# Six matmuls on a zero tile, in three places of the opening of a fused SSM-convolution and SwiGLU kernel

## The chip, the cores and the metric

The kernel runs on one core of a Trainium2 chip. A core has a matmul engine (PE), a vector engine (DVE), an activation engine (ACT), a general one (POOL), a queue engine for DMAs (SP), an on-chip memory of 128 partitions, and a small accumulator memory (PSUM) that PE writes and DVE and ACT read. The metric is the device time of one execution in microseconds. It was measured in four runs: median 284.02 us, from 283.33 to 284.58.

## The reference

Inputs are bfloat16; the sequence has 2048 rows of 640 channels. Cut to what matters:

```python
x = A_q
q = layernorm(x)
k_shift = sum over t in 0..3 of k[row - t] * shift_k[:, t]      # a causal filter with four taps
kv = k_shift * v
y = irfft(rfft(kv, 4096) * rfft(ssm_k, 4096))[:2048]           # a causal convolution along the rows
h = x + q * (y + kv * ssm_D)
n = layernorm(h)
out = h + (silu(n @ w_gate) * (n @ w_up)) @ w_down              # inner width 1728
```

## The kernel before, in words

The 2048 rows are worked on as four blocks of 512 (NB, MB), the 640 channels as the free dimension. The long convolution is done block by block with trigonometric transforms written as matmuls: the filter blocks are transformed by WG (g_transform), the products kv by WX (x_transform), pairs of transformed blocks are multiplied on DVE (pair), and WI goes back (inverse). Each block then goes through layernorm and the feed-forward part (ffn).

The kernel builds a list of operations, each with an engine, what it reads and writes, and a function that issues its instructions (Plan.add). Operations are numbered in the order in which the code adds them. The list SEQUENCE, written out in full, gives the order in which they are issued. Each engine works through its own operations in that order; between engines, an instruction waits for those it depends on. PSUM is split into two pools, A and F, of two buffers each (psA, psF), each of two banks; an operation with acq takes the buffer that was released longest ago, and one with rel gives it back.

What happens in the opening, with its lines:

- Line 278 clears the tile junk (the same memory as hl[0]) on DVE, and warm (lines 282 to 290) issues five matmuls 128x512 on it, then one DVE copy of a single element that reads the result.
- wcast (lines 321 to 329), four times: two matmuls each spread one row of the four-tap filter over all partitions, into pool A, and ACT copies the result to w4.
- gload(0) (line 302 on): the first filter block is loaded, and transposed by PE as matmuls against an identity (line 314), five to a group, four groups, in pool F; ACT copies each group out (line 316).
- front_first (line 379 on), for each tile of 128 rows of the first block: DVE multiplies k by the four filter rows (line 383), PE adds up the shifted rows with band matrices, the taps (line 393), into pool A, and for the first two tiles turns v around (line 401). DVE multiplies both (lines 404, 406). SP's loads of the next block's k come into tiles that the taps read, and so wait for them.
- g_transform(0) (line 344) and x_transform(0) (line 433) follow on PE.

The fixed junk matmul that exists already is this line:

```python
nc.tensor.matmul(ps(g)[:, i % 2, :], junk[:, 0:P], junk[:, 0:MB], start=True, stop=True)
```

Of the kernel before, what the change touches and what calls it, by code (L numbers as in the profile page):

```python
# [18 lines left out]
P = 128  # L19
MB = 512  # L20
# [34 lines left out]
class Plan:  # L55
# [7 lines left out]
    def add(self, eng, dur, fn, r=(), w=(), pr=0, acq=None, rel=None, kb=0, after=(), t0=0.0, lag=0.0):  # L63
        deps = set()
        for k in r:
            if k in self.writer:
                deps.add(self.writer[k])
        for k in list(w) + list(after):
            if k in self.writer:
                deps.add(self.writer[k])  # L70
            deps |= self.readers.get(k, set())
        i = len(self.ops)
        self.ops.append(dict(eng=eng, dur=dur, fn=fn, deps=deps, pr=pr, acq=acq and acq[0], rel=rel and rel[0], group=(acq or rel or (0, 0))[1], kb=kb, w=list(w), t0=t0, lag=lag, stage=self.stage))
        for k in r:
            self.readers.setdefault(k, set()).add(i)
        for k in w:
            self.writer[k], self.readers[k] = i, set()
        return i

    def order(self):  # L80

        assert sorted(SEQUENCE) == list(range(len(self.ops)))
        spare = {name: list(range(k)) for name, k in self.pools.items()}
        for i in SEQUENCE:
            o = self.ops[i]
            if o["acq"]:
                self.held[o["group"]] = spare[o["acq"]].pop(0)
            if o["rel"]:
                spare[o["rel"]].append(self.held[o["group"]])
        return SEQUENCE  # L90

# [10 lines left out]
BACK = "SSSS"  # L102
TRANS = {1: 0, 2: 0, 3: 0}
WARM = (0.43, 5, 0)
SEQUENCE = [int(i) for i in """
2 19 10 7 0 8 20 5 1 3 24 21 22 71 34 4 11 72 199 13 207 12 23 14 15 17 16 73 18 25 27 26 28 29 31 51 30 32 56 52 53 61 58 54 57 59 55 230 74 64 76 62
77 60 6 75 33 206 65 63 198 78 69 79 35 66 43 67 36 80 68 37 44 208 81 90 98 209 45 91 70 82 99 85 210 92 38 83 100 46 86 93 39 229 101 94 200 40 102
95 41 201 96 89 42 202 47 103 97 104 106 48 148 105 203 49 211 149 214 109 215 172 220 50 88 107 204 173 164 205 108 174 165 150 175 110 231 156 232
111 112 221 151 216 114 157 113 158 222 115 116 212 132 217 118 119 159 190 218 223 133 160 219 191 117 213 224 152 120 161 225 136 192 121 441 153
326 226 130 315 193 122 228 434 162 131 314 227 134 433 182 135 163 137 123 256 183 166 138 248 124 167 139 194 233 125 141 184 195 140 257 154 249  # L110
128 185 126 258 129 142 155 181 250 9 186 127 143 243 168 187 196 443 169 259 176 251 146 435 147 197 260 177 252 261 144 327 188 180 145 253 178 189
436 442 170 444 179 234 245 262 254 171 316 445 263 242 235 317 236 437 321 246 318 322 319 338 446 237 244 328 339 323 324 329 438 238 320 449 247
439 255 333 330 325 331 334 239 350 265 335 345 336 351 332 264 346 340 337 266 347 399 348 341 362 440 456 240 268 342 447 363 343 352 448 267 278
353 269 293 272 270 294 357 273 349 276 271 358 374 359 455 344 274 360 375 430 354 355 364 275 429 365 356 369 279 366 277 367 361 370 280 371 387
386 368 299 376 398 281 450 372 451 388 377 284 400 285 381 373 452 378 432 382 379 282 389 380 283 457 295 383 453 384 390 458 296 286 391 394 459
570 392 385 402 454 297 403 300 569 460 395 401 298 396 558 287 301 404 675 289 393 302 410 291 290 397 461 303 411 431 667 305 292 412 306 462 413
304 477 491 405 492 307 478 414 493 406 494 415 308 499 480 407 495 500 417 496 481 312 497 408 310 416 418 483 313 423 557 87 409 479 311 424 465 482
425 485 426 501 427 419 484 420 486 559 421 498 560 84 464 489 561 564 562 487 502 565 566 581 463 563 503 669 567 582 576 466 467 488 577 571 568 507
578 579 572 593 504 668 670 468 583 676 580 594 573 509 505 574 584 470 575 471 510 588 585 589 490 605 586 428 506 600 422 590 587 606 671 591 508
601 469 595 472 592 511 473 596 672 597 515 474 684 512 598 683 536 617 516 618 513 602 673 607 674 475 603 514 608 537 519 612 604 599 521 677 517  # L120
630 685 538 518 609 613 610 522 520 539 686 619 614 631 611 629 615 523 620 621 678 540 624 524 542 616 625 622 679 541 626 680 632 627 623 689 709
525 799 633 634 527 628 681 543 812 637 635 710 690 528 800 648 811 544 638 639 636 649 545 526 640 650 691 548 651 549 641 529 692 652 687 546 530
642 688 693 547 711 643 534 644 550 694 532 655 653 551 535 712 682 645 656 533 695 654 696 657 646 714 739 661 740 713 555 741 553 556 662 531 647
715 742 731 554 716 663 732 733 552 717 743 734 664 744 658 241 718 665 735 697 659 745 666 719 801 746 736 802 721 803 737 804 806 720 698 807 823
805 808 723 813 809 824 699 722 814 700 818 725 815 816 819 835 810 817 820 825 724 836 821 702 826 822 827 727 830 828 738 829 831 701 847 726 842
848 832 728 833 843 703 834 837 729 844 845 838 704 859 846 747 839 854 860 840 660 841 849 856 749 705 855 872 730 871 850 857 851 706 858 861 852
873 750 862 853 309 707 288 863 866 748 864 867 868 865 751 874 869 910 753 875 876 755 752 877 922 759 879 763 754 777 756 921 909 708 870 757 778
476 880 779 758 881 760 764 780 761 883 762 781 782 767 765 884 768 766 786 882 878 885 785 783 771 784 769 886 787 890 770 788 773 887 774 891 772
789 888 775 892 790 776 893 791 897 793 894 889 792 895 898 795 796 899 794 896 797 900 798 903 901 904 905 906 916 907 917 918 911 919 920 912 913
933 923 914 934 915 924 925 928 926 927 929 930 945 940 931 946 932 941 942 935 943 944 936 937 957 952 938 958 939 953 954 947 955 956 948 949 969  # L130
964 950 970 951 959 960 961 982 981 965 908 962 966 963 976 967 983 902 968 977 978 989 979 980 971 990 991 972 973 984 974 975 985 992 986 993 987
988 994 995 996 999 997 1000 998 1001 1005 1002 1006 1003 1007 1004 1008 1011 1009 1010 1014 1012 1013 1015 1016
""".split()]


# [9 lines left out]
def kernel(  # L145
# [14 lines left out]
    nc = tc.nc  # L160
# [60 lines left out]
    junk = hl[0]  # L221
# [27 lines left out]
    A = [slot[6], slot[7], slot[1], slot[3]]  # L249
# [6 lines left out]
    def ps(group):  # L256
        return ps_of[group[0]][plan.held[group]]

    add = plan.add
# [22 lines left out]
    def warm(name, n, pr, r=()):  # L282

        g = ("F", name)

        def mm():
            for i in range(n):
                nc.tensor.matmul(ps(g)[:, i % 2, :], junk[:, 0:P], junk[:, 0:MB], start=True, stop=True)
        add("PE", n * WARM[0], mm, r=["hl0", *r], w=[g], pr=pr, acq=("F", g))
        add("DVE", 0.1, lambda: nc.vector.tensor_copy(junk[0:1, 0:1], ps(g)[0:1, 0, 0:1]), r=[g], w=["hl0"], pr=pr, rel=("F", g))  # L290

    if WARM[1]:
        warm("a", WARM[1], -300)
    add("POOL", 0.1, lambda: nc.gpsimd.memset(ones[:], 1.0), w=["ones"], pr=-99)
    add("POOL", 0.1, lambda: nc.gpsimd.memset(mhalf[:], -0.5), w=["mhalf"], pr=-9)
    add("POOL", 0.1, lambda: nc.gpsimd.memset(eps[:], EPS), w=["eps"], pr=-9)
# [24 lines left out]
    def wcast(t):  # L321
        g = ("A", "w", t)
        src = wrow.rearrange("p (d j) -> p j d", j=4)

        def mm():
            for h in range(2):
                nc.tensor.matmul(ps(g)[:, h, 0:NH], ones[:], src[:, 3 - t, h * NH:(h + 1) * NH], start=True, stop=True)
        add("PE", 0.5, mm, r=["ones", "wrow"], w=[g], pr=-9, acq=("A", g))
        add("ACT", act(D), lambda: nc.scalar.copy(r3(w4[:, t, :]), ps(g)[:, :, 0:NH]), r=[g], w=["w4"], pr=-9, rel=("A", g))

    for t in range(4):
        wcast(t)
    if WARM[2]:
        warm("b", WARM[2], -70, r=[("A", "w", 3)])

# [502 lines left out]
```

## Time and profile before

| what | value |
|---|---|
| median of four runs | 284.02 us |
| profiled execution | 284.52 us |
| its span, first to last instruction | 282.4 us |
| PE busy | 271.3 us (96%) |
| DVE busy | 218.8 us (77%) |
| ACT busy | 208.1 us (74%) |
| POOL busy | 37.3 us (13%) |
| DMA, mean over the span | 156 GB/s, 44.13 MB |

The page is of one profiled execution. Times in it are microseconds from the first instruction, and the profiled execution's own time is longer than its span by 2.1 us, which lies around the instructions. A line of the timeline gives start, length, engine, line of the code, operation, what it writes and reads, how many instructions are merged, and in brackets how long the engine was idle before and what ended it. Matmuls overlap in the pipeline, so the spacing of their starts says how fast PE works, not the length of one. The chain that ended last is followed back from the last instruction, at each step to what released it.

### The profile page before, as it was taken

Reading aid. Unit: us, or ns where it says so; the run is one execution under the profiler, and the core shown is the slowest. Engines: PE = TensorE matmul, PEld = TensorE weight load, DVE = VectorE, ACT = ScalarE, POOL = GpSimd, SP = SyncE. Lnnn points to the kernel's source line nnn. Section 1 sums busy time; section 2 is a strip of 40 time slices with the busy share of each in tenths; the row PEclk is TensorE's granted clock in tenths of the full one; section 3 lists DMA queues with packets and bytes.
Section 4 is the critical chain, followed back from the end, with each engine's and each line's share of the span. In section 5 each row is a group of like instructions: output and inputs, shape, how many; then the busy total and the mean of one; then the engine's idle time right before and its main releaser. Section 6 shows DMA issues by size and latency. Waiting matters only on the chain.

```text
span 282.4 us, 4392 instructions
## 1 busy us (share of the span) xinstructions
PE 271.3 (96%) x1617; PEld 160.2 (57%) x1631; DVE 218.8 (77%) x295; ACT 208.1 (74%) x408; POOL 37.3 (13%) x34
## 2 busy tenths in 40 slices
PE   6899999999999989999999999999999999999995
PEld 2567776776445447664455476644446774444673
DVE  1669999999999999999999998999997710211212
ACT  4597789899968799828989997888859964546300
POOL 3304000110210020840010025000210230000000
PEclk9999999999999999999999999999999999999999
DMA  6959590945495669575685543635645071655011
GB/s 178 391 189 269 149 298 18 316 129 116 108 303 155 188 206 272 135 162 163 167 261 133 173 132 70 186 95 145 170 103 142 11 104 51 164 147 158 0 46 50
DMA packets 69114, 44.13 MB, mean 156 GB/s; under 512 B 28322, under 2 KB 66787, under 8 KB 68964
## 3 DMA queue, kind: packets, MB, share of 16 engines
q1 hardware_dynamic: 68370, 41.68, 53.9%
q0 software_dynamic: 576, 1.97, 2.3%
q8 instruction: 13, 0.21, 0.3%
q10 hardware_dynamic: 146, 0.20, 0.2%
q14 instruction: 9, 0.07, 0.1%
HBM read 36.63 MB, written 2.62 MB: 139 GB/s over the span
## 4 chain that ended last, share of the span: by engine, by line
PE 51%; DVE 28%; ACT 10%; DMA 5%; issue 5%; SPq 1%; ACTq 0%; DVEq 0%
PE psF L685 24%; PE psF L736 12%; DVE s L443 10%; DVE T L443 7%; PE psF L344 3%; PE psA L393 3%; PE psA L597 3%; PE psA L433 3%; DMA x<-in_A_k_dram 2%; DMA wu<-in_B_w_up_dram 2%; DVE k L361 2%; ACT junk L530 2%; ACT uc L697 2%; PE psF L714 1%; ACT junk L527 1%
## 5 line engine op out<-in xcount | busy, mean ns | idle before, releaser
L685 PE MATMUL psF<-hT,wg 128*128 128x512 bf16 x271 | 68.4, 379 | 1.2 <-ACT uc L697 0.5
L685 PE MATMUL psF<-hT,wu 128*128 128x512 bf16 x255 | 63.5, 379 | 1.6 <-DMA wu<-in_B_w_up_dram 1.4
L736 PE MATMUL psF<-wd,tT 128*128 128x320 bf16 x420 | 60.5, 299 | 0.0
L736 PEld LDWEIGHTS <-tT 128*128 128x128 bf16 x420 | 41.1, 98 | 16.1
L443 DVE TENSOR_TENSOR T<-s,s 128x2560 bf16<-128x2560 bf16 x32 | 47.2, 1485 | 0.1
L443 DVE TENSOR_TENSOR s<-s,T 128x2560 bf16<-128x2560 bf16 x32 | 46.9, 1485 | 0.1
L685 PEld LDWEIGHTS <-wg 128*128 128x128 bf16 x280 | 27.2, 98 | 32.6 <-issue 2.1
L699 DVE TENSOR_TENSOR tT<-sg,uc 128x512 bf16<-128x512 bf16 (+1 forms) x56 | 23.2, 420 | 28.7 <-ACT uc L697 28.7
L550 POOL TENSOR_TENSOR rstd<-var,mhalf 128x2 f32<-128x2 f32 (+2 forms) x15 | 20.8, 1389 | 178.4 <-ACT var L531 149.1
L690 ACT ACTIVATE sg<-psF 128x512 bf16<-128x512 f32 (+1 forms) x56 | 33.4, 597 | 14.6 <-PE psF L685 8.3
L685 PEld LDWEIGHTS <-wu 128*128 128x128 bf16 x260 | 25.3, 98 | 31.9 <-DMA wu<-in_B_w_up_dram 2.0
L697 ACT CAST uc<-psF 128x512 bf16<-128x512 f32 (+1 forms) x56 | 32.8, 586 | 9.6 <-PE psF L685 9.5
L344 PEld LDWEIGHTS <-s 128*128 128x128 bf16 x256 | 25.0, 98 | 10.3 <-issue 0.3
L344 PE MATMUL psF<-wd,s 128*128 128x320 bf16 x192 | 28.6, 299 | 0.1
L346 ACT CAST s<-psF 128x640 bf16<-128x640 f32 x32 | 21.5, 695 | 6.4 <-PE psF L344 6.3
L530 ACT ACTIVATE junk<-x,sm 128x640 uint8<-128x640 bf16 x28 | 23.4, 834 | 0.5
L433 PE MATMUL psA<-kv,WX 128*128 128x320 bf16 x128 | 21.3, 299 | 0.8 <-DVE kv L422 0.7
L438 ACT CAST s<-psA 128x640 bf16<-128x640 f32 x29 | 19.5, 704 | 3.1 <-PE psA L433 3.1
L443 DVE TENSOR_TENSOR s<-s,s 128x2560 bf16<-128x2560 bf16 x14 | 20.7, 1484 | 0.0
L527 ACT ACTIVATE junk<-x 128x640 uint8<-128x640 bf16 x28 | 20.6, 738 | 0.0
L597 PE MATMUL psA<-s,WI 128*128 128x320 bf16 x128 | 19.2, 299 | 0.7 <-DVE s L443 0.4
L361 DVE TENSOR_TENSOR k<-k,w 128x2560 bf16<-128x2560 bf16 x12 | 17.6, 1484 | 0.1
(78 smaller groups left out, 261.2 us busy)
## 6 DMA issues: line engine op xcount, KB each, us to landing
k<-in_A_k_dram SPq DMA_DIRECT2D x12, 640.0 KB, 5.2
wg<-in_B_w_gate_dram SPq DMA_DIRECT2D x24, 320.0 KB, 3.6
wu<-in_B_w_up_dram SPq DMA_DIRECT2D x24, 320.0 KB, 3.8
v<-in_A_v_dram SPq DMA_DIRECT2D x12, 160.0 KB, 4.1
wd<-in_B_w_down_dram SPq DMA_DIRECT2D x3, 640.0 KB, 7.4
out_dram<-o SPq DMA_DIRECT2D x9, 160.0 KB, 3.1
s<-const_wg SPq DMA_DIRECT2D x1, 1024.0 KB
x<-in_A_q_dram SPq DMA_DIRECT2D x3, 320.0 KB, 6.6
```

The costliest lines, as they stand in the source:

```text
L344: nc.tensor.matmul(ps(g)[:, h, 0:NH], WG[:, kt, ct * P:(ct + 1) * P], gT[p][:, kt, h * NH:(h + 1) * NH], start=(kt == 0), stop=(kt == 3))
L361: add("DVE", dve(4 * D), lambda: nc.vector.tensor_mul(kd[:], kd[:], w4[:]), r=["w4"] + ks, w=[kn], pr=pr)
L433: nc.tensor.matmul(ps(g)[:, h, 0:NH], WX[:, kt, ct * P:(ct + 1) * P], kv[:, base + kt, h * NH:(h + 1) * NH], start=(kt == 0), stop=(kt == 1))
L443: add("DVE", dve(n * D), lambda: f(o, a, b), r=ks(ak) + ks(bk), w=ks(ok), after=["WG0", "WG1"] if ok[:2] == "s7" else [], pr=pr)
L527: add("ACT", 0.74, lambda: nc.scalar.activation(junks[j][:], src, ACT.Copy, scale=-1.0 / D, accum_out=s[:, 0:1]), r=[xk], w=[k + "a", f"ju ...
L530: nc.scalar.activation(junks[j][:], src, ACT.Square, bias=s[:, 0:1], accum_out=s[:, 1:2])
L597: nc.tensor.matmul(ps(g)[:, h, 0:NH], WI[:, 4 * part + ct, m * P:(m + 1) * P], a[part][:, ct, h * NH:(h + 1) * NH], start=(ct == 0), stop= ...
L685: i = nc.tensor.matmul(ps(gr)[:, which, :], w[:, kt, cc * P:(cc + 1) * P], hT[b][:, kt, :], start=(kt == 0), stop=(kt == 4))
L690: apart(gr, 0, nc.scalar.activation(sg[s][:z, :], ps(gr)[:z, 0, :], ACT.Silu))
L697: add("ACT", act(MB), lambda gr=gr, s=s, z=z, merged=merged: nc.scalar.copy(uc[s][:z, :], ps(gr)[64:128, 0, :] if merged else ps(gr)[:, 1, ...
L699: add("DVE", dve(MB), lambda c=c, s=s, z=z: TM(tT[:z, c * MB:(c + 1) * MB], sg[s][:z, :], uc[s][:z, :]), r=[f"sg{s}", f"uc{s}"], w=[f"tT{c ...
L736: nc.tensor.matmul(ps(gr)[:, h, 0:NH], tT[:, c * MB + m * P:c * MB + (m + 1) * P], wd[:, c, h * NH:(h + 1) * NH], start=(c == 0 and not re ...
```

## The change

A new function fill(name, n) adds one operation on PE of n matmuls 128x512 on the zero tile junk, into a buffer of pool A that it takes and releases itself. It reads the key "hl0", so it comes after the copy of warm. No operation reads the result. It is called three times, for two, one and three matmuls. The new operations get the numbers 5, 6 and 7, so that every later number in SEQUENCE is greater by three; apart from this the order is the same, with the three put in at these places (the operations around them are named by what they are):

- 5, "before the transposes": behind the four wcast groups on PE, ahead of the first group of transposes (28)
- 6, "between them": behind the second group of transposes (30), ahead of the third (32)
- 7, "before the taps": behind the fourth group of transposes (34), ahead of the taps of the first tile (55)

```diff
 WARM = (0.43, 5, 0)
+FILLS = [("before the transposes", 2), ("between them", 1), ("before the taps", 3)]
 SEQUENCE = [int(i) for i in """
...
+    def fill(name, n):
+
+        g = ("A", name)
+
+        def mm():
+            for i in range(n):
+                nc.tensor.matmul(ps(g)[:, i % 2, :], junk[:, 0:P], junk[:, 0:MB], start=True, stop=True)
+        add("PE", n * WARM[0], mm, r=["hl0"], w=[g], pr=-200, acq=("A", g), rel=("A", g))
+
+    for name, n in FILLS:
+        fill(name, n)
```

The beginning of the order, before and after (cut from the two lists):

```
before: ... 11 72 199 13 207 12 23 14 15 17 16 73 18 25 27 26 28 29 31 51 30 32 56 52 ...
after:  ... 14 75 202 16 210 15 26 17 18 20 19 76 21 5 28 30 29 31 6 32 34 54 33 35 59 7 55 ...
```

## The prediction

> **What bounds the kernel now.** I read the chain that ended last first, limited to the opening, then the instructions of PE in order of time. The chain's first 36 us (start, length, what):
>
> ```profile
> 2.00 7.06 DMA x<-in_A_k_dram
> 9.15 1.50 DVE k L383
> 10.70 2.29 PE psA L393 x8
> 12.99 1.07 PE psF L401 x4
> 14.06 6.40 PE psA L393 x42
> 20.46 3.26 PE psF L344 x24
> 23.72 1.09 PE psA L433 x8
> ...
> 34.62 0.70 ACT s L346
> 35.35 1.49 DVE T L443
> ```
>
> The load of k and one DVE product set when the first tap can start (10.66). From there PE alone sets the time: the taps (L393) and two flips (L401) run without a hole from 10.70 to 20.46. Later DVE takes over. Before 10.70, PE waits for data. PE in order of time:
>
> ```profile
> 1.67 2.31 PE L288 MATMUL psF<-hl 128*128 128x512 bf16 x5 [1.67 <-DVE hl L278]
> 3.92 1.29 PE L327 MATMUL psA<-T,ones 1*128 1x320 bf16 x4
> 5.42 1.31 PE L327 MATMUL psA<-T,ones 1*128 1x320 bf16 x4 [0.21 <-ACT w L329]
> 7.00 1.25 PE L314 MATMUL psF<-perm,tT 128*128 128x128 bf16 x10 [0.27 <-DMA tT<-in_A_ssm_k_dram]
> 8.50 1.29 PE L314 MATMUL psF<-perm,tT 128*128 128x128 bf16 x10 [0.25 <-ACT wd L316]
> 10.70 2.29 PE L393 MATMUL psA<-k,perm 128*128 128x320 bf16 x8 [0.91 <-DVE k L383]
> ...
> 16.49 0.71 PE L393 MATMUL psA<-s,perm 128*128 128x320 bf16 x4
> ```
>
> The brackets show three waits in the opening: 0.27 before the transposes, 0.25 between them, 0.91 before the taps. The fills go into these. The second thing to see is speed. Eight taps of 320 columns take 2.29 us at 10.70: from tap to tap about 0.267 us. The 24 matmuls of 320 columns at 20.46 take 3.26 us: 0.136 each. So PE runs at half rate in the opening. The clock column of the slices doesn't show this: it reads full from the start. The line view of the taps does (min/median/max ns):
>
> ```profile
> L393 PE MATMUL psA<-k,perm x28: 299/344/474, 10.7 to 18.3; 128*128 128x320 bf16 x28
> L393 PE MATMUL psA<-s,perm x22: 299/299/299, 16.5 to 20.2; 128*128 128x320 bf16 x22
> ```
>
> The switch lies between these. Check: taps and flips are 54 matmuls, at 0.1365 that is 7.37 us of fast work; they took 9.76. With a switch at T, (T - 10.70)/2 + (20.46 - T) = 7.37 gives T = 15.5. The trace's own clock record, which no view prints, begins at 15.36. So some 4.7 us of tap work runs slow, and 2.3 us of the path is lost to it. That is the only thing that this change can win.
>
> **What makes PE fast: the rule and the row.** [...] the record from 15.36 is 266.24 us long, 78 times 3.413; so the windows before it ended at 11.94, 8.53 and 5.12. PE was busy all through 11.94 to 15.36. It was not busy all through 8.53 to 11.94 (waits of 0.9 and less: about 70% busy), and wasn't released. The window 1.71 to 5.12 is awkward: nearly full of work (five matmuls on zeros to about 3.9, then four with one row of weights), and it released nothing. Either the one-row matmuls or the zeros count for little; the row can't tell which. That is the main doubt below. [...]
>
> **The change part by part.** Nothing is removed; each added matmul is 128x512 on the zero tile. Its nearest row is L288: five in 2.31 us, start to start 0.427 slow. Nobody reads the results, so no evictions and no DMAs are added; every queue keeps its order, and PE alone gets three extra steps.
>
> *Two ahead of the transposes.* They take a psA buffer. The order of releases makes it that of the third weight broadcast, freed by its ACT copy:
>
> ```profile
> 6.18 1.29 ACT L329 CAST w<-psA 128x640 bf16<-128x640 f32 x2 [0.21 <-PE psA L327]
> ```
>
> The first of the two takes 0.69, so it is free at 6.87, and PE starts some 0.06 later (as at 8.50 after a copy that ended at 8.44): 6.93. Two by 0.427 ends at 7.78. The transposes could have begun at 7.00, when their data came: they are 0.78 late.
>
> *One between them.* The second pair of transposes waits for the ACT copies, which also move by 0.78. From first transpose to third it was 8.50 - 7.00 = 1.50; ten transposes take ten times 0.107 = 1.07, plus the fill's 0.427 is again 1.50. So it costs nothing: 7.78 + 1.50 = 9.28 for the third. Cover gone (ACT faster), it would cost 0.43. The last transpose follows its copy, as now, with a hole of about 0.06, and they end at 10.41 instead of 9.63.
>
> *Three behind.* Slow, 10.41 + 3 x 0.427 = 11.69. The product was ready at 10.66, so the taps start at 11.69 instead of 10.70: **0.99 late**. Were the clock fast already, three would take about 0.65 (at half the slow spacing).
>
> *The cost alone.* Late by 0.99, with the switch where it was: the extra time runs in what was slow time, so it costs half: finish = 7.37 + T/2 + start/2, and 0.99/2 = +0.50.
>
> *The gain.* PE is now busy from 6.93 on with nothing longer than 0.06 empty. Before, this began at 10.70. The difference, 3.77, is more than a window, so whatever the phase, the first full window ends one window earlier, and in (3.77 - 3.41)/3.41 = about 10% of the phases two. In this trace's phase the window 8.53 to 11.94 is full, and T moves from 15.36 to 11.94: 3.41/2 = -1.71. **Sum: -1.71 + 0.50 = -1.21** for the end of the taps: 20.46 goes to about 19.2. Ends for the unknown: +2.2 (the fills count for nothing and a late start misses one more window, 0.50 + 1.71) to -2.9 (two windows). I take -1.21, because a matmul over all rows is what filled the window that did release the clock.
>
> *Who could hold it back.* DVE makes the fourth product at 15.03 behind the first reversed product at 14.29, which waits for ACT's y. With fast flips y comes some 0.15 earlier, and the fourth product ends at about 16.35. The fourth tile's taps are wanted at 19.19 - 14 x 0.1365 = 17.28: cover of 0.9. The second reversed product then frees their buffer at about 17.2, just in time. After the taps come the two L406/L421/L422 steps of DVE, then this:
>
> ```profile
> 18.59 0.80 SPq L274 DMA_DIRECT2D k<-in_A_k_dram  x2
> ...
> 23.16 1.49 DVE L361 TENSOR_TENSOR k<-k,w 128x2560 bf16<-128x2560 bf16 x1
> ```
>
> SP's load of the next k waits for the third tile's taps and lands 4.5 us later, at 23.09, just when DVE is free (23.04). Those taps end at about 17.3 instead of 18.4, so the load moves by 1.1 to 1.2, nearly as much as DVE. The transposing loads behind it on SP move along. From 23.16 DVE has hardly a hole to 58, so the shift is carried on. The chain shows no waiting for a clock of its own behind that, only work and loads released by work. **So -1.2 at the end.** Against the profiled execution (284.52 around a span of 282.4) that is 283.3; the median of the runs stands 0.50 lower, 284.02, and gives **282.8**.
>
> **The rivals.** Anything within 0.3% (0.85 us) is about what a measurement of this kernel can't tell from no change.
>
> *Two windows earlier* (9%): the phase is kind, 1.71 more: 281.1.
>
> *The fills don't count* (17%). The window 1.71 to 5.12 speaks for it. Also narrow transposes might count for less, and they fill 1.45 of the 3.41 us. Then T stays and only the delay is left: 284.5.
>
> *The clock comes a window later* (12%), the one that ends slower. If the fills don't count, the first full window must begin at 11.69, not 10.70. Where a boundary falls in that 0.99 us, 29% of phases, it is missed: +0.50 + 1.71 = +2.2, 286.2. Against it: in the trace's phase the boundary is at 11.94, just 0.25 behind the new start. That is little room; a delay of over 1.24 decides it, so the chance is more than the product of the two.
>
> *The gain is eaten later* (10%). At 94.70 a string of SP loads begins, and a weight load of 6.44 us is on the chain there. If it is held by something that doesn't move, half the gain is left: 283.4 to 284, say 283.5.
>
> **How the numbers follow.** One window earlier has 52%, with its own range of 282.2 to 283.4 (phases scatter: the four runs lie 1.25 apart, and a switch anywhere in a window of 3.41 is worth up to 1.7). Of it, 45 are faster by over 0.3% and 7 within. With 9 of two windows and 4 of the eaten gain, faster is 0.58; 7, 15 of the uncounted fills and 6 of the eaten gain are within: 0.28; the rest, 12 and 2, slower: 0.14. The range leaves out most of the two-window case below and the late window above: 281.4 to 285.0.
>
> **What would show it.** Right: transposes at about 7.8 and 9.3, taps from about 11.7, of which nearly all at 299 ns; the end of taps near 19.2; the next k load issued near 17.4; DVE's L361 near 22.0; the chain behind it the same. Wrong: taps at 474 ns until 15 or later (fills don't count), or L361 at 22.0 and the span unchanged (eaten later), or a first tap well behind 11.7 (a wait of the fills that I missed).

## The result, and the profile after

The changed kernel takes 283.06 us (median of 42 runs, 281.64 to 284.67); the kernel before, measured beside it, 284.16 us (63 runs, 282.75 to 285.49). The ratio is 0.9964, 95% interval 0.9954 to 0.9974: 1.02 us faster. A second set of runs of the same kernel gave 0.9955 (0.9934 to 0.9975). The profiled execution took 283.18 us around a span of 281.1.

PE in order of time after the change (start, length, engine, line, operation, count, idle before); lines 302, 327, 406 and 414 are the fills, transposes, taps and flips:

```profile
6.92 1.01 PE L302 MATMUL psA<-hl 128*128 128x512 bf16 x2 [0.18 <-ACT w L342]
7.72 1.27 PE L327 MATMUL psF<-perm,tT 128*128 128x128 bf16 x10
8.79 0.64 PE L302 MATMUL psA<-hl 128*128 128x512 bf16 x1
9.24 1.29 PE L327 MATMUL psF<-perm,tT 128*128 128x128 bf16 x10
10.33 1.00 PE L302 MATMUL psA<-hl 128*128 128x512 bf16 x3
11.16 1.25 PE L406 MATMUL psA<-k,perm 128*128 128x320 bf16 x8
12.25 0.71 PE L414 MATMUL psF<-hT,perm 128*128 128x320 bf16 x4
...
18.50 3.42 PE L357 MATMUL psF<-wd,s 128*128 128x320 bf16 x24
```

The waits are gone from 6.92 on. The first eight taps take 1.25 us where they took 2.29: all of them run fast, 0.136 us from start to start (11.16 to 12.25 for eight) where it was 0.26 (10.70 to 12.78). The trace's clock record (the times at which it notes the granted clock) begins at 10.70, inside the three fills, where it began at 15.36 before. At full rate it is 269.653 us long, before 266.240: 79 and 78 times 3.413, and 3.413 apart. A stretch of that length, counted from the start of a profile's record, is called a window below; windows ahead of a record are worked out so. The taps end 1.80 us earlier: the row behind them starts at 18.50, and before the change it was

```profile
20.30 3.42 PE L344 MATMUL psF<-wd,s 128*128 128x320 bf16 x24
```

The chain that ended last, in the opening, and DVE's wait at its end:

```profile
10.53 0.80 PE psA L302 x3
11.33 1.09 PE psA L406 x8
12.42 0.54 PE psF L414 x4
12.96 3.82 PE psA L406 x28
16.79 5.08 DMA k<-in_A_k_dram
21.89 1.50 DVE k L374
```

```profile
16.79 0.81 SPq L275 DMA_DIRECT2D k<-in_A_k_dram  x2
...
20.42 0.82 DVE L435 TENSOR_TENSOR kv<-kv,rev 128x1280 bf16<-128x1280 bf16 x1
21.89 1.49 DVE L374 TENSOR_TENSOR k<-k,w 128x2560 bf16<-128x2560 bf16 x1 [0.65 <-DMA k<-in_A_k_dram]
```

Here something new is on the chain. The load of the next k goes out 1.80 us earlier, but takes 5.08 us where it took 4.50, and DVE, free at 21.24, waits 0.65 us for it. So 1.80 us on the taps became 1.27 us at this step (23.16 to 21.89), and the span is 1.3 us shorter (282.4 to 281.1): behind this product nothing more was lost between these two profiles. The two records begin 4.66 us apart, which is no whole number of windows (1.36), so the two profiles do not stand at the same phase, and the 1.02 us of the many runs is the size of the change.

### The profile page after: what moved, and what is told of

The parts are those of the page before. It is cut to its first block, busy times and chain, and to the rows that moved or that the text cites. A ratio compares the mean times of both kernels' runs of the same rounds, so it can differ in the third digit from the quotient of the medians.

```text
span 281.1 us, 4404 instructions
## 1 busy us (share of the span) xinstructions
PE 271.5 (97%) x1623; PEld 159.9 (57%) x1637; DVE 218.4 (78%) x295; ACT 207.7 (74%) x408; POOL 37.9 (13%) x34
## 4 chain that ended last, share of the span: by engine, by line
PE 39%; DVE 31%; ACT 17%; issue 8%; DMA 3%; POOL 1%; POOLq 0%; ACTq 0%; DVEq 0%
PE psF L698 22%; DVE s L456 11%; DVE T L456 7%; PE psF L749 7%; ACT junk L543 3%; DVE k L374 3%; ACT uc L710 2%; ACT junk L540 2%; ACT xln L573 2%; PE psA L610 2%; ACT sg L703 2%; DMA k<-in_A_k_dram 2%; PE psA L406 2%; DVE k L379 2%; DVE tT L712 2%
## 5 line engine op out<-in xcount | busy, mean ns | idle before, releaser
L610 PE MATMUL psA<-s,WI 128*128 128x320 bf16 x128 | 19.2, 299 | 0.9 <-DVE s L456 0.6
```

The source lines that it names most:

```text
L610: nc.tensor.matmul(ps(g)[:, h, 0:NH], WI[:, 4 * part + ct, m * P:(m + 1) * P], a[part][:, ct, h * NH:(h + 1) * NH], start=(ct == 0), stop= ...
```

## The experiments

The author's theory: the fills win because matmuls over all rows, on zeros too, fill a window earlier, and full rate follows. Where full rate follows a window, that window is said to open the clock, and to count. Rivals: zeros or fills count for nothing; part of the six would do; the gain is eaten later. Every kernel below computes the whole reference. Besides the lines shown, the fills' numbers are put into the order list at the places named, and fill takes the pool as a third value, "A" where the lines don't show one. The kernel before was measured again beside each group of kernels.

### What fills a window

Sixteen opening matmuls on zeros instead of five, no fills:

```diff
-WARM = (0.43, 5, 0)
+WARM = (0.43, 16, 0)
```

> Sixteen opening matmuls on zeros instead of five, no fills; this only asks what fills a window. Sixteen at 0.427 would run from 1.67 to 8.5. My theory (matmuls over all rows count, zeros or not): the first full window ends between 5.1 and 8.5, the spacing falls from 0.427 to 0.216 inside this row of sixteen, and transposes and taps are fast from the first. Rival (zeros don't count): all sixteen at 0.427, and the switch comes 3.4 us or more behind the first transposes, as before near 14 to 17.

And the same sixteen on one row of the tile:

```diff
-                nc.tensor.matmul(ps(g)[:, i % 2, :], junk[:, 0:P], junk[:, 0:MB], start=True, stop=True)
+                nc.tensor.matmul(ps(g)[:, i % 2, :], junk[0:1, 0:P], junk[0:1, 0:MB], start=True, stop=True)
```

> As the sixteen zeros, but each opening matmul takes one row of the tile instead of 128. If one-row matmuls fill a window as well, the spacing falls to 0.216 inside the sixteen, between 5.1 and 8.5. If they don't (my theory, from the window 1.71 to 5.12 before, which was nearly full and released nothing), all sixteen stay at 0.427 and the switch comes only 3.4 us behind full-row work.

PE in order of time with sixteen zeros, then its windows (stretch, its length, busy time of PE, PEld, DVE, ACT and POOL with counts, granted clock, DMA share, GB/s):

```profile
1.67 6.27 PE L295 MATMUL psF<-hl 128*128 128x512 bf16 x16 [1.67 <-DVE hl L285]
7.87 1.29 PE L334 MATMUL psA<-T,ones 1*128 1x320 bf16 x4
9.38 1.31 PE L334 MATMUL psA<-T,ones 1*128 1x320 bf16 x4 [0.21 <-ACT w L336]
10.62 1.25 PE L321 MATMUL psF<-perm,tT 128*128 128x128 bf16 x10
```

```profile
3.00:7.00 4.00, 4.00 (x11) 1.45 (x10) 0.00 (x0) 0.07 (x1) 2.20 (x2) 1.00 0.87 251
7.05:10.47 3.42, 3.21 (x12) 0.93 (x10) 0.15 (x1) 1.62 (x3) 0.00 (x0) 1.00 1.05 386
10.47:13.88 3.41, 3.16 (x24) 2.56 (x24) 2.43 (x2) 3.22 (x6) 0.66 (x1) 0.50 1.07 396
```

PE in order of time with sixteen one-row matmuls:

```profile
1.67 7.00 PE L295 MATMUL psF<-hl 1*128 1x512 bf16 x16 [1.67 <-DVE hl L285]
...
13.82 2.34 PE L400 MATMUL psA<-k,perm 128*128 128x320 bf16 x8
15.96 0.98 PE L408 MATMUL psF<-hT,perm 128*128 128x320 bf16 x4
```

Each of the two ran once (284.71 and 286.50 us, with 283.80 for the kernel before beside them), so their traces are read and not their times.

Behind the first zeros the clock opened: its record begins at 7.05, inside the row, and the sixteen end sooner than the one-row ones (6.27 against 7.00 us), as the theory had it. Not as expected, the clock closed again: the row of 10.47 reads 0.50. It did so after 3.42 us, and the half rate lasted 3.41, one window each. In the window before it closed, counted from start to start, PE had 0.73 us of zeros and then only one-row broadcasts, some 2.2 us. From 13.88 on the record reads 1.00. So transposes ran slow after all. But they count: the window that ended at 13.88 was filled by them (2.1 us) and the first taps. Sixteen one-row matmuls didn't open it: PE was busy with them and the broadcasts through two windows of its phase (2.85 to 6.27 and 6.27 to 9.68), and the record begins at 16.50, behind the first window that transposes and taps had filled (13.09 to 16.50). That bears on the doubt about the window 1.71 to 5.12 before: no window of one-row work opened the clock here, and one of zeros alone did (3.64 to 7.05). The zeros filled only some 61% of the window before.

### The delay without the clock

The change, with its fills on one row:

```diff
-                nc.tensor.matmul(ps(g)[:, i % 2, :], junk[:, 0:P], junk[:, 0:MB], start=True, stop=True)
+                nc.tensor.matmul(ps(g)[:, i % 2, :], junk[0:1, 0:P], junk[0:1, 0:MB], start=True, stop=True)
```

> The change with its six fills on one row of the zero tile: the same places, the same time on PE, the same waits. If one-row matmuls don't count for the clock, only the delay of the taps (0.99 us, half of it lost) is left, and 29% of the phases lose a window more: +0.50 + 0.29 x 1.71 = +1.0 us, ratio 1.0035 (1.001 to 1.005). If they count, or if the gain has nothing to do with the clock: as the change, 0.9964.

Measured: 285.79 us (5 runs), ratio 1.0067 (1.0050 to 1.0083), 1.9 us slower. The sign is the expected one, the size more. PE in order of time:

```profile
10.76 1.46 PE L309 MATMUL psA<-hl 1*128 1x512 bf16 x3
12.14 2.31 PE L413 MATMUL psA<-k,perm 128*128 128x320 bf16 x8
14.25 1.27 PE L421 MATMUL psF<-hT,perm 128*128 128x320 bf16 x4
15.32 3.26 PE L413 MATMUL psA<-k,perm 128*128 128x320 bf16 x14
```

The taps start at 12.14, 1.44 us late and not 0.99: at each of the five switches between one-row and full-row work PE had 0.09 to 0.13 us more between two starts than the change run again at half rate (below; its taps start at 11.61), 0.53 in all. The prediction's formula with 1.44 gives 0.72 + 0.42 x 1.71 = 1.4, the lower edge of what was measured. The record begins at 17.74, and the first eight taps are 0.26 us from start to start (12.14 to 14.25). From start to start, PE had work for 85% and 96% of the two windows ahead of the one that opened the clock (7.50 to 10.91 and 10.91 to 14.33). Full-row work was 61% and 64% of them, the rest one-row, and neither opened it. This is the slower rival, made real: the same places and nearly the same time on PE, but full rate only from 17.74.

### Parts of the six

Three fills alone, two alone, one and two, and five in holes that they fit (two of these in pool F, whose buffers are free then):

```diff
-FILLS = [("before the transposes", 2), ("between them", 1), ("before the taps", 3)]
+FILLS = [("before the taps", 3)]                               # last three
+FILLS = [("before the transposes", 2)]                         # first two
+FILLS = [("between them", 1), ("before the taps", 2)]          # one and two
+FILLS = [("between the broadcasts", 1, "F"), ("before the transposes", 1, "F"),
+         ("between them", 1, "A"), ("before the taps", 2, "A")]   # free five
```

> Only the three fills ahead of the taps. Transposes at 7.00 as before, PE busy from there but for a hole of 0.25 at 8.25 and one of 0.06; slow, the taps start at 10.91 instead of 10.70. If a hole of 7% leaves a window counted: busy from 3.7 us earlier than before, -1.71 + 0.10 and a second window in 8% of the phases, -1.7 on the taps, of which the later stages keep some 0.7 as they did of the change: -1.2 us, ratio 0.9957, better than the change. If the window must be whole, busy from 8.50: 64% of the phases win it, -0.7 us, ratio 0.9975. If it needs the two ahead of the transposes: near +0.1, ratio 1.000.

> Only the two fills ahead of the transposes. Transposes at 7.78 to 10.41 with the old hole of some 0.25 to 0.4 between the pairs, then a hole of 0.29 until the product is there: taps at 10.70, no delay. About 18% of a window from 6.93 on is empty. If a window may be 18% empty, this gains what the change gains without paying 0.50: -1.7 us on the taps, 0.7 of it kept, ratio 0.9957. If it may not, only windows from about 8.9 on count: half the phases win one, -0.6 us, ratio 0.998.

> One fill between the transposes and two ahead of the taps, none ahead of the transposes: transposes at 7.00, taps at 10.70, nothing delayed, 8% of the time from 7.00 empty. Busy from 3.7 us earlier than before: one window in all phases, two in 8%: -1.85 us on the taps, of which 0.7 is kept, -1.3 us, ratio 0.9955: a little better than the change. If what counts is that the two ahead of the transposes are there: no gain beyond that of the three alone, 0.9975.

> Five fills, each in a hole that it fits, in buffers of the other pool where those of the first are still read: one between the second and third weight broadcast, one ahead of the transposes at 6.49, one between them, two ahead of the taps. Nothing is delayed; full-row work without a hole over 0.2 from 6.49 on, 4.21 us earlier than before: one window in 77% of the phases, two in 23%: -2.1 us on the taps, -1.5 us kept, ratio 0.9948, better than the change. If an earlier clock is worth nothing more because DVE's products or the load of the next k set the pace: no better than the one above, 0.9955 to 0.9965.

> The change as it is, beside the three that follow on one chip: ratio 0.9964 again (0.995 to 0.998). Its clock record should begin at another moment than 10.70, anywhere from about 10 to 13.7, and the span should follow it by about half a microsecond for each.

| kernel | median us | ratio to before, interval | lowest, highest |
|---|---|---|---|
| last three | 283.27 | 0.9975 (0.9956 to 0.9994) | 281.50, 285.12 |
| first two | 283.47 | 0.9972 (0.9951 to 0.9994) | 281.32, 285.37 |
| one and two | 282.58 | 0.9947 (0.9926 to 0.9968) | 281.81, 283.80 |
| free five | 282.84 | 0.9955 (0.9931 to 0.9978) | 281.81, 283.55 |
| the change again | 282.68 | 0.9955 (0.9934 to 0.9975) | 281.58, 284.75 |

Three fills with nothing delayed (one and two) come out no worse at the centre than the six. The free five were expected to win by their earlier start; they didn't show it. In their profile the fill ahead of the transposes starts at 6.90 and not at 6.49, as the fill between the broadcasts had pushed the next broadcasts from 5.42 to 5.68; the record begins at 11.11, no earlier than the change's; and the chain runs over DVE's products, for which the last taps wait until 16.71. That is the limit that their expectation named. Between these three kernels the intervals decide nothing. Either half of the change alone gains less at its centre and spreads wider, but the intervals overlap here too. In the profile of the first two, PE was empty between the transposes and before the taps:

```profile
9.24 1.29 PE L334 MATMUL psF<-perm,tT 128*128 128x128 bf16 x10 [0.25 <-ACT wd L336]
10.91 2.29 PE L413 MATMUL psA<-k,perm 128*128 128x320 bf16 x8 [0.38 <-DVE k L403]
```

Its record begins at 14.50, so the window 7.67 to 11.09 did not count. Counted from start to start of the matmuls, which leaves out the pipeline's tail that the brackets leave in (a fast tap takes 299 ns, and the next starts 136 ns behind it), 0.45 + 0.59 and a gap of 0.11 were empty in it: 1.15 of 3.41, 34%. In the window 10.47 to 13.88 of the sixteen zeros about 0.69 was empty, 20%, and it did count. The emptiest window that counted stands in the profile of one and two with the early k (next section), whose record begins at 9.74:

```profile
7.00 1.25 PE L334 MATMUL psF<-perm,tT 128*128 128x128 bf16 x10 [0.26 <-DMA tT<-in_A_ssm_k_dram]
8.04 0.63 PE L309 MATMUL psA<-hl 128*128 128x512 bf16 x1
8.49 1.29 PE L334 MATMUL psF<-perm,tT 128*128 128x128 bf16 x10
9.57 0.68 PE L309 MATMUL psA<-hl 128*128 128x512 bf16 x2
10.97 1.25 PE L413 MATMUL psA<-k,perm 128*128 128x320 bf16 x8 [0.71 <-DVE k L403]
```

Of its window, 6.33 to 9.74, only what lies behind 7.00 was full-row work, with small gaps: some 77%. In the fourteen profiles of this case each window at half rate with 77% or more of full-row work opened the clock; of those that didn't, the fullest is the 66% of the first two. In between none was measured. The expectation of 18% empty for the first two was measured with the tail and too kind. For the last three, holes of 0.45 and 0.11 (16%) are fewer than the 23% of a window that counted, which spoke for 0.9957; the centre is 0.9975, and the interval holds both. That one stays open.

The change run again shows one way in which an execution loses the gain. The chain, and DVE:

```profile
17.27 6.12 DMA k<-in_A_k_dram
23.42 1.50 DVE k L374
```

```profile
23.42 1.49 DVE L374 TENSOR_TENSOR k<-k,w 128x2560 bf16<-128x2560 bf16 x1 [1.69 <-DMA k<-in_A_k_dram]
```

The record began at 11.67 there, and the row behind the taps started at 18.98, 1.3 us earlier than before; but the load of k took 6.12 us, DVE's product came at 23.42, later than the 23.16 of before, and the span was 282.6. The whole gain was gone in that execution, and the half microsecond that was expected of the later clock was 1.5. DVE waited for this load in the profiles of last three (0.64 us) and of one and two (0.45 us) as well, but not in those of first two and of the free five.

### The load of k

The second tile's products are put into memory that is free at that time, so that SP's first load of the next k need not wait for the third tile's taps, and goes out right behind the large filter load:

```diff
-    products, prodk = [k4[0], k4[1], slot[4][0], slot[4][1]], ["k4_0", "k4_1", "s4c", "s4s"]
+    products, prodk = [k4[0], slot[1][0], slot[4][0], slot[4][1]], ["k4_0", "s1c", "s4c", "s4s"]
```

Once without fills, then with the change's six, with one and two, and with the free five:

> The kernel before, without fills, but the second tile's products lie in other memory, so that SP's first load of the next block's k has nothing to wait for and goes out behind the large load at 6.6 instead of behind the third tile's taps at 18.59. Control for the next three. Before, that load landed at 23.09 and DVE was free at 23.04, so by that profile it gives nothing; but its landing varies from 4.4 to 6.2 us over the profiles, so on average perhaps -0.3 us: ratio 0.999 (0.997 to 1.001).

> The change with the early k. If the wait for k is what ate part of the gain (0.65 us in one profile of the change, 1.69 in another), DVE's L361 follows its neighbour without a wait near 21.3, and the gain is what the sum gave for the taps, -1.4 us, and what the control gains: ratio 0.994 (0.992 to 0.996), with fewer slow runs than the change has. If the gain was lost elsewhere: as the change, 0.9964, the control's own gain added.

> One fill between and two before the taps, nothing delayed, with the early k: -1.85 us on the taps and no wait for k: ratio 0.993 (0.991 to 0.995). If the wait for k isn't what eats the gain: 0.9947 as without it.

> The five fills in their holes with the early k: -2.1 us on the taps, nothing waits for k: ratio 0.9925 (0.9905 to 0.9945), the best of all. If an earlier clock is held up by DVE's products, no better than the one above.

| kernel | median us | ratio to before, interval | lowest, highest |
|---|---|---|---|
| no fills, early k | 283.89 | 0.9990 (0.9970 to 1.0010) | 282.76, 285.30 |
| the change, early k | 282.49 | 0.9939 (0.9918 to 0.9960) | 281.97, 283.25 |
| one and two, early k | 282.29 | 0.9947 (0.9923 to 0.9971) | 281.69, 283.77 |
| free five, early k | 282.79 | 0.9937 (0.9917 to 0.9957) | 281.67, 283.55 |

DVE in the change with the early k:

```profile
20.62 0.82 DVE L442 TENSOR_TENSOR kv<-kv,rev 128x1280 bf16<-128x1280 bf16 x1
21.36 1.48 DVE L381 TENSOR_TENSOR k<-k,w 128x2560 bf16<-128x2560 bf16 x1
```

The wait is gone: the product follows its neighbour. It starts 0.53 us earlier than in the change (21.36 against 21.89), at nearly the same moment of the clock (11.10 against 10.70). The span of this profile is 279.9, 1.2 us less than the change's; the other 0.6 us came later: from the start of this product on, the span still takes between 258.2 and 259.2 us over the fourteen profiles. None of its 10 runs is above 283.3 us, against 23 of the change's 59. The centre moved from 0.9964 to 0.9939 where the control moved by 0.001. The direction fits, and it is shown that the wait goes; the two intervals still touch. And one and two didn't move at all (0.9947 with and without the early k), which is what its expectation gave for the case that this wait isn't what eats the gain. Of its runs, 3 of 11 are above 283.3 us, without the early k 4 of 12. The free five moved from 0.9955 to 0.9937, not to the expected 0.9925. So how much of the missing gain the load held is not settled.

With the clock open early, other limits come first. In the profiles of one and two and of the free five with the early k, PE waited 0.71 and 0.64 us for DVE's first product ahead of the taps. In the second of these DVE's first product waited for the first load of k until 10.64 (9.15 before), and the taps began only at 12.19. The loads behind the early k on SP's queue move forward too, so it is the whole group of loads that was tried. The five versions with undelayed taps, an early k or both beat the kernel before by 0.45% to 0.63%; their centres lie at or below those of the change (0.9964 and 0.9955), but none is shown to beat it.

## Why the prediction was right, and where its sum was off

The forecast of 282.8 with 281.4 to 285.0 held: 283.06. Point by point:

- **The bound** was read rightly: half-rate taps on the path, some 2.3 us to win, and a clock column that hides it. (The column can show the half rate, as the 0.50 above; ahead of the record it reads 1.00, as in 14.00 to 15.00 before, though the four flips just ahead of that, 12.78 to 13.85, are 0.267 us from start to start.)
- **The delay.** Transposes were put at 7.78 and 9.28, measured 7.72 and 9.24. Taps were put at 11.69 for a slow clock: 11.61 in the profile whose clock opened at 11.67, 11.16 where it opened at 10.70.
- **The clock.** 'PE is now busy from 6.93 on' was right, and so was counting on full-row zeros. (The 'about 70% busy' of the window 8.53 to 11.94 was read with the pipeline's tails; from start to start it is 64%.) The 3.41 us that the sum takes for a window is what the two records differ by (3.413), and what full and half rate lasted with sixteen zeros (3.42 and 3.41). That a full window of work brings full rate, in whatever phase, was the author's estimate there; the experiments show it for the windows named above. That the switch comes a window earlier in the same phase can't be read from two single profiles, since the phase differs; but the records of the two profiles of the change begin at 10.70 and 11.67, those of the other kernels with fills both between the transposes and before the taps between 9.74 and 12.94 (five profiles), and those without fills at 15.36 and 15.31. The one-row fills, with ratio 1.0067 and a record from 17.74 in the same places, show that it is the clock and not the fills' place.
- **The end of the taps** was put at about 19.2 for a switch at 11.94; by the same formula it is 19.05 for 11.67, where they ended near 19.15.
- **The step that was off** is 'lands 4.5 us later, at 23.09, just when DVE is free'. The load's 4.5 us was taken as fixed. It took 5.08 and 6.12 us in the two profiles of the change, and DVE waited 0.65 and 1.69 us. The prediction saw that load and DVE meet within 0.05 us, and yet let the whole 1.2 us pass. Its rival 'the gain is eaten later' had the right kind of cause in the wrong place: it looked at 94.70, and it happens at 22.
- **Luck.** 'L361 near 22.0' was met by 21.89 because two differences cancel: the load went out at 16.79 and not near 17.4, as the clock opened at 10.70, and took 0.58 us longer to land than before. The forecast of -1.2 stood against -1.02, near to it in part because the two-window phases, which its sum left out, weigh the other way (some 0.17 on the mean; argued, not shown).
- **A rival's sum.** 'Two windows earlier' takes 2.9 us off the median, 284.02, though the reading had put only 2.3 us of the path at stake. The 2.9 holds for an execution whose clock would have opened late, near 17.3 without the fills, and such an execution stands above the median. Measured from the median, 281.1 is too low.

## What to carry to other kernels

To have PE fast early, look at how full its work is, and by what. In this case full rate followed windows with 77% or more of matmuls that use all rows, on zeros too, and half rate followed a window in which PE had work for 96% of the time, but such matmuls for only 64%. A few matmuls whose result nobody reads, put into holes ahead of the critical matmuls, gained here; a block of sixteen at the very start opened the clock, which closed again behind the one-row work that followed (half rate from 10.47 to 13.88), and pushed the first tap to 13.20. Fills sized to their holes (one and two) gave no less at their centre than the six that delay the taps. When a stage is pulled forward, the loads that it releases can become the next limit: where a load and its reader meet within a tenth of a microsecond, take the load's spread (here 4.50 to 6.12 us for one load), not its one landing, into the sum.

## What the runs showed of the hardware that was not expected

- No window that was filled up by one-row matmuls opened the clock: behind windows with 92% (before), 85% and 96% (the one-row fills) of work from start to start, with 61% to 64% of full-row work in them, PE stayed at half rate. Nor did one-row matmuls hold it open in the one profile that shows it: full rate from 7.05 to 10.47 with sixteen zeros, half until 13.88, with 0.73 us of zeros and some 2.2 us of one-row broadcasts in the window before it closed.
- A window with 23% of it not full-row work counted (one and two with the early k), one with 34% did not (the first two).
- The row of four one-row broadcasts takes 1.29 us with the clock recorded at full (7.87, sixteen zeros) as it does ahead of the record (3.92, before, behind zeros 0.427 us from start to start), so its length doesn't show the clock. Why is open.
- The full-rate record is a whole number of windows long before and after the change (78 and 79 times 3.413 us: 266.240 and 269.653), and begins at a moment that differs between two executions of the same kernel: 10.70 and 11.67 for the change.
- The same load of 640 KB, released by the same taps, took 4.50 us to land before, 5.07 us with the last three fills, and 5.08 and 6.12 us in two profiles of the change.
